# Gated delta rule and softplus block: head-pair transposes, one product for keys and queries, PSUM banks by head parity, a planner with instruction blocks, another order of loads

## Chip, cores, metric

The kernel runs on one core of a Trainium2 chip. The metric is device time in microseconds (us), the median of several executions. The engines are TensorE (PE in the profile, PEld for its weight loads), VectorE (DVE), ScalarE (ACT), GpSimd (POOL) and SyncE (SP, here only issuing DMAs). The kernel before gave 360.08 us.

## The reference

A recurrence over 768 steps for 32 heads (4 batches of 8) of width 48, then a two-layer block with softplus over all 3072 rows. Cut to what matters:

```python
B, H, S, D = 4, 8, 768, 48
k_n = k / (np.linalg.norm(k, axis=-1, keepdims=True) + 1e-06)
for t in range(S):
    y[:, :, t] = g[:, :, t] * einsum('bhd,bhde->bhe', q[:, :, t], state)
    v_old = einsum('bhde,bhd->bhe', state, kt)
    state = state + bt * einsum('bhd,bhe->bhde', kt, vt - v_old)
x = y.transpose(0, 2, 1, 3).reshape(3072, 384)
h = x @ w_in                                   # 384 -> 2048
out = (maximum(h, 0) + log1p(exp(-abs(h)))) @ w_out   # 2048 -> 384
```

## The kernel before

The sequence is cut into 6 chunks of 128 steps, each into two of 64. In a chunk: keys are normalised; keys and queries are transposed per head; products of keys with keys (for a triangular solve) and of keys with queries (for the output) are formed; a short solve runs on VectorE (first chunk) or POOL; then the recurrence over the sub-chunks, and the dense block. The order of instructions on every engine comes from a list scheduler inside the kernel ("the planner"), which is given a cost for each item.

Each matmul of the products keeps a stationary tile of 48 rows and 32 or 64 columns:

```python
def trs(...):                                   # 32 transposes of 64x64
    for j, x in ((0, a), (1, b)):               # keys, queries
        for h in range(H):
            for b2 in range(2):
                r = slice(64 * b2, 64 * b2 + 64)
                nc.tensor.transpose(o[r, h, j, :], x.ap[r, p, h, :], ident[r, r])

def kkmm(x=kqt[gi], kkp=kkp):                   # 48 matmuls, all with 32 columns
    for h in range(H):
        for b2 in range(2):
            ...
            ka, kb = x.ap[r, h, 0, :32], x.ap[r, h, 0, 32:]
            nc.tensor.matmul(o[ra, :, h, :], ka, x.ap[r, h, 0, :])   # L470
            nc.tensor.matmul(o[rb, 0, h, :], kb, kb)                 # L471
            nc.tensor.matmul(o[rb, 1, h, :], kb, ka)                 # L472

def kqmm(x=kqt[gi], mp=mp):                     # 16 matmuls, all with 64 columns
    for h in range(H):
        for b2 in range(2):
            nc.tensor.matmul(o[64 * b2 : 64 * b2 + 64, h, :],
                             x.ap[r, h, 0, :], x.ap[r, h, 1, :])     # L504
```

There are 4 such groups in a chunk, 24 in all. The two dense products are `h <- xt, w_in` (L908) and `o <- ga, w_out` (L940).

## Time and profile before

| | before |
|---|---|
| time | 360.08 us (360.02 to 362.51) |
| span of the profiled execution | 362.2 us |
| TensorE busy, matmuls | 274.1 us, 8416 |
| of these in the 24 product groups | 1152 + 384 matmuls, 0.55 and about 0.4 us a group (first start to the start of what follows; median of the groups that stand alone) |
| waits of over 0.25 us at every 128th matmul | 28, 44.9 us |
| first dense matmul | at 88.7 us |

A row of the profile's groups gives line, engine, operation, out<-in by name, stationary rows*columns, shape and count; after the first bar the time in which at least one of the group ran and the mean length of one; after the second the engine's idle time before them and who ended it. A matmul's length includes latency that overlaps with its neighbours, so what a matmul costs is read from start to start. The prediction says how the waits at every 128th matmul were found. Times of a group are measured everywhere as in the table.

### The profile page before, as it was taken

Reading aid. Unit: us, or ns where it says so; the run is one execution under the profiler, and the core shown is the slowest. Engines: PE = TensorE matmul, PEld = TensorE weight load, DVE = VectorE, ACT = ScalarE, POOL = GpSimd, SP = SyncE. Lnnn points to the kernel's source line nnn. Section 1 sums busy time; section 2 is a strip of 40 time slices with the busy share of each in tenths; the row PEclk is TensorE's granted clock in tenths of the full one; section 3 lists DMA queues with packets and bytes.
Section 4 is the critical chain, followed back from the end, with each engine's and each line's share of the span. In section 5 each row is a group of like instructions: output and inputs, shape, how many; then the busy total and the mean of one; then the engine's idle time right before and its main releaser. Section 6 shows DMA issues by size and latency. Waiting matters only on the chain.

```text
span 362.2 us, 17913 instructions
## 1 busy us (share of the span) xinstructions
PE 274.1 (76%) x8416; PEld 175.7 (49%) x8416; DVE 148.1 (41%) x280; ACT 148.9 (41%) x233; POOL 104.5 (29%) x196
## 2 busy tenths in 40 slices
PE   0351035669996897779999978985899978999984
PEld 0341034657454466435666445654565544565442
DVE  2825924239442256314566451661056330441011
ACT  3330233442775214446735674241456324541620
POOL 6400060054830892000528987000006600000000
PEclk9985555555997599569999998995599998999999
DMA  7999985714740136562416701362000011011012
GB/s 138 188 193 169 184 147 107 136 29 91 133 92 5 25 78 124 110 116 48 89 27 127 161 4 27 69 122 59 6 4 5 24 46 25 4 25 45 22 28 59
DMA packets 106473, 27.98 MB, mean 77 GB/s; under 512 B 100768, under 2 KB 106016, under 8 KB 106400
## 3 DMA queue, kind: packets, MB, share of 16 engines
q1 hardware_dynamic: 103680, 23.60, 34.0%
q0 software_dynamic: 2720, 3.24, 5.2%
q8 instruction: 65, 1.06, 1.3%
q14 instruction: 8, 0.07, 0.1%
HBM read 25.26 MB, written 4.72 MB: 83 GB/s over the span
## 4 chain that ended last, share of the span: by engine, by line
PE 71%; issue 13%; DVE 7%; ACT 5%; SPq 2%; DMA 1%; DVEq 0%; ACTq 0%
PE o L940 19%; PE h L908 19%; PE d L436 5%; PE d L752 4%; PE d L732 2%; PE d L504 2%; SPq L262 2%; ACT td L618 2%; PE d L657 2%; PE d L470 2%; PE d L637 2%; PE d L691 2%; PE d L813 2%; PE d L790 2%; PE d L824 2%
## 5 line engine op out<-in xcount | busy, mean ns | idle before, releaser
L908 PE MATMUL h<-xt,w_in 128*128 128x512 f16 x288 | 80.8, 410 | 0.8 <-DVE xt L863 0.4
L940 PE MATMUL o<-w_out,ga 128*128 128x384 f16 x384 | 75.5, 336 | 4.8 <-DVE osb L953 4.2
L922 ACT ACTIVATE ga<-h 128x512 f16<-128x512 f32 x96 | 56.8, 598 | 52.7 <-PE h L908 51.1
L744 DVE TENSOR_TENSOR w<-vf,d 128x384 f16<-128x384 f32 x48 | 25.8, 550 | 67.2 <-PE d L769 63.5
L940 PEld LDWEIGHTS <-ga 128*128 128x128 f16 x384 | 35.5, 99 | 30.6 <-issue 8.1
L368 POOL TENSOR_TENSOR ss<-ss,half_c 128x32 f32<-128x32 f32 x5 | 27.4, 5487 | 59.7 <-DVE ss L329 59.7
L761 ACT CAST u<-d 128x384 f16<-128x384 f32 x48 | 22.2, 479 | 47.9 <-PE d L752 47.9
L908 PEld LDWEIGHTS <-w_in 128*128 128x128 f16 x288 | 25.5, 102 | 27.6 <-issue 8.0
L953 DVE COPY osb<-o 128x384 f32<-128x384 f32 x24 | 13.4, 557 | 55.7 <-PE o L940 55.7
L582 POOL TENSOR_TENSOR tt<-tt,tmp 128x30 f32<-128x30 f32 (+7 forms) x75 | 29.5, 393 | 5.9
L575 POOL TENSOR_TENSOR tmp<-nn,tt 128x30 f32<-128x30 f32 (+7 forms) x75 | 28.7, 382 | 5.9
L523 DVE TENSOR_TENSOR mt<-d,mask 128x512 f16<-128x512 f32 x24 | 16.4, 683 | 29.2 <-PE d L504 29.2
L453 ACT COPY kqt<-d 128x1024 f16<-128x1024 f16 x24 | 23.8, 1014 | 9.2 <-PE d L436 9.1
L436 PE MATMUL d<-ident,kn 64*64 64x64 f16 x384 | 13.5, 219 | 17.5 <-DVE kn L389 13.9
L564 POOL TENSOR_TENSOR nn<-ln,nbeta_l 128x256 f32<-128x256 f16 x10 | 6.0, 619 | 67.4 <-DVE ln L541 67.4
L752 PE MATMUL d<-w,td 32*32 32x48 f16 x1152 | 19.4, 191 | 6.3 <-issue 4.7
L488 ACT CAST kk<-d 128x512 f16<-128x512 f32 x24 | 14.1, 586 | 23.3 <-PE d L472 23.2
L752 PEld LDWEIGHTS <-td 32*32 32x32 f16 x1152 | 14.4, 96 | 18.2 <-issue 15.3
L637 PE MATMUL d<-ident,td 32*32 32x16 f16 x768 | 7.4, 172 | 19.2 <-ACT td L618 17.7
L436 PEld LDWEIGHTS <-kn 64*64 64x64 f16 x384 | 10.6, 131 | 21.5 <-DVE kn L389 13.9
L799 DVE TENSOR_TENSOR s<-d,s 128x384 f16<-128x384 f32 x22 | 12.0, 553 | 16.4 <-PE d L790 16.4
L637 PEld LDWEIGHTS <-td 32*32 32x32 f16 x768 | 6.7, 90 | 20.8 <-ACT td L618 18.5
(69 smaller groups left out, 398.2 us busy)
## 6 DMA issues: line engine op xcount, KB each, us to landing
kf<-in_k_dram SPq DMA_DIRECT2D x24, 192.0 KB, 4.7
qf<-in_q_dram SPq DMA_DIRECT2D x24, 192.0 KB, 4.8
vf<-in_v_dram SPq DMA_DIRECT2D x24, 192.0 KB, 4.4
gf<-in_g_dram SPq DMA_DIRECT2D x24, 192.0 KB, 4.9
out_dram<-osb SPq DMA_DIRECT2D x48, 96.0 KB, 2.2
w_in<-in_moe_w_in_dram POOLq DMA_DIRECT2D x1, 1536.0 KB, 12.2
w_out<-in_moe_w_out_dram POOLq DMA_DIRECT2D x1, 1536.0 KB, 22.9
beta_l<-in_beta_dram POOLq DMA_DIRECT2D x8, 12.0 KB, 3.8
```

The costliest lines, as they stand in the source:

```text
L368: lambda ss=ss: nc.gpsimd.tensor_tensor(ss.ap, ss.ap, half_c, ALU.pow)
L436: nc.tensor.transpose(o[r, h, j, :], x.ap[r, p, h, :], ident[r, r])
L453: lambda tp=tp, o=kqt[gi]: nc.scalar.copy(o.ap.rearrange("p h j t -> p (h j t)"), f16ps(tp.ap))
L575: eng.tensor_tensor(t, nn.ap[:, :, j + 1 :, j : j + 1].broadcast_to([P, 2, n, w]), tt.ap[:, :, j : j + 1, 16 : 16 + w].broadcast_to([P, 2, ...
L582: eng.tensor_tensor(rows, rows, t, ALU.add)
L637: nc.tensor.matmul(uv(np_.ap)[r, u], td.ap[r, u, :], ident[r, 32 * qd : 32 * qd + 16],)
L744: nc.vector.tensor_tensor(o.ap, vf.ap[:, p], hd(wp.ap), ALU.subtract)
L752: nc.tensor.matmul(hd(up.ap)[r, h], td_.ap[r, u0 + 2 * h, :], o.ap[r, h],)
L761: nc.scalar.copy(o.ap, hd(up.ap))
L908: nc.tensor.matmul(hp.ap, w_in[:, j, f * P : (f + 1) * P], xt.ap[:, j, :], start=(j == 0), stop=(j == 2),)
L922: lambda hp=hp, o=gb_: nc.scalar.activation(o.ap, hp.ap, AF.Softplus)
L940: nc.tensor.matmul(op.ap[:, :DM], ga[f].ap[:, 128 * gi : 128 * gi + 128], w_out[:, f, :], start=(f == 0), stop=(f == NF - 1),)
```

## The change

Its intent is fewer instructions on TensorE. Keys and queries are transposed two heads at a time (8 transposes of 128x128 instead of 32). One matmul then gives the products of keys with keys and with queries; a second, with 32 columns, overwrites a part of its lower half. Since the two heads of a pair lie in different row halves, their products go to two PSUM banks. A second correction in the recurrence is folded into a new product z, a transposition by TensorE goes to VectorE. The planner counts matmuls in blocks of 128. The core of the diff, cuts marked with `...`, the comments behind `#` added here:

```diff
+                        for i in range(NP):
+                            nc.tensor.transpose(
+                                o[:, i, :, j],
+                                x.ap[:, p, 2 * i : 2 * i + 2].rearrange("p h d -> p (h d)"),
+                                ident,
+                            )
...
-                            nc.tensor.matmul(o[ra, :, h, :], ka, x.ap[r, h, 0, :])
-                            nc.tensor.matmul(o[rb, 0, h, :], kb, kb)
-                            nc.tensor.matmul(o[rb, 1, h, :], kb, ka)
...
+                def gram(kq=kq, gp=gp):
+                    for i in range(NP):
+                        for r in range(2):
+                            for m in range(2):
+                                x = kq.ap[FEAT[m], 2 * i + r]
+                                o = gp[m].ap.rearrange("p (i c) -> p i c", i=NP)
+                                nc.tensor.matmul(o[HALF[r], i], x[:, C:], x)        # L531
+                                o = gp[m].ap.rearrange("p (i x c) -> p i x c", i=NP, c=HC)
+                                nc.tensor.matmul(                                  # L535
+                                    o[QUAD[2 * r + 1], i, 0:3:2], x[:, C + HC :], x[:, C:]
+                                )
+                t2 = add("PE", 0.4, gram, ..., mm=32)
...
+            if e == "PE":
+                block = issued // self.BLOCK            # 128 matmuls
+                issued += it.mm
+                end = it.end
+                while issued // self.BLOCK > block:
+                    block += 1
+                    end = max(end, arrive[block])
+                    arrive.append(end + self.FETCH)     # 3.5 us
...
     load("k", k, r_k, 0)
-    for cc in range(NSS):
+    load("q", q, r_q, 0)
+    load("k", k, r_k, 1)
+    load("v", v, r_v, 0)
+    weights()                                          # w_in, planned after v of chunk 0
+    load("g", g, r_g, 0)
+    load("q", q, r_q, 1)
+    weights2()
...
```

## The prediction

> **What bounds the kernel now.** I read the page first, then the groups by line, the waits, the timeline of TensorE and the stage table.
>
> ```profile
> PE 274.1 (76%) x8416; PEld 175.7 (49%) x8416; DVE 148.1 (41%) x280; ACT 148.9 (41%) x233; POOL 104.5 (29%) x196
> q8 instruction: 65, 1.06, 1.3%
> PE 71%; issue 13%; DVE 7%; ACT 5%; SPq 2%; DMA 1%; DVEq 0%; ACTq 0%
> ...
> L908 PE MATMUL h<-xt,w_in 128*128 128x512 f16 x288 | 80.8, 410 | 0.8 <-DVE xt L863 0.4
> L940 PE MATMUL o<-w_out,ga 128*128 128x384 f16 x384 | 75.5, 336 | 4.8 <-DVE osb L953 4.2
> ```
>
> TensorE holds 71% of the chain that ended last, and another 13% (47 us) is "issue": it waits for nothing the profile shows. No other engine is busy for half of the span, so TensorE's stream is the bound. Only 672 of its 8416 matmuls are the dense ones (L908, L940). At their usual spacing in the trace (216 and 163 ns from start to start) these need 288 x 216 + 384 x 163 ns = 125 us; the remaining 7744 are small.
>
> What "issue" is shows in the timeline of TensorE from 46 to 58 us (start, length, group, count, wait before it):
>
> ```profile
> 51.52 0.66 PE L657 MATMUL d<-tn,kk 16*32 16x16 f16 x65 [2.12 <-issue]
> 52.01 0.62 PE L680 MATMUL d<-td,ident 32*32 32x512 f16 x4
> 52.92 0.59 PE L691 MATMUL d<-td,xs 32*16 32x16 f16 x59 [0.29 <-ACT xs L668]
> 55.52 0.67 PE L691 MATMUL d<-td,xs 32*16 32x16 f16 x69 [2.00 <-issue]
> 56.99 0.78 PE L752 MATMUL d<-w,td 32*32 32x48 f16 x59 [0.80 <-ACT td L704]
> ```
>
> From one "issue" wait to the next are 65 + 4 + 59 = 128 matmuls, and the wait falls in mid-group, where no data can be the reason. I numbered all weight loads: the long waits of this kind fall on number 96 modulo 128, 28 of them over 0.25 us, 44.9 us in sum. Each such block of 256 instructions goes with one packet of the instruction queue (65 packets). Blocks of small matmuls alone take 3.5 to 4.0 us however little they compute; a block with 10 or more dense matmuls has no wait.
>
> Before the steady state there is a slow start. The waits put 13.9 us down to the first normalised keys and 15.4 us to the first triangular solve on VectorE, and the first dense matmul starts only at 88.7 us.
>
> **What the Trainium skill says.** "Advanced Engine Details and Errata", section ISA Cache: lines of 16 KB, 256 instructions, two of them (it also gives TensorE more memory, which would not explain these waits). The trace agrees with the line: 1.06 MB / 65 = 16 KB, and 2 x 8416 / 256 = 65.75. "TensorEngine Tiling (Array Packing)", Key Properties: changing the tiling mode drains the array. The trace agrees: from L472 (32 columns) to L504 (64 columns) the starts are 102 to 115 ns apart every time, while L813 follows L790 (both 64 by 64) after 28 ns. Same page, Gotcha 1: different row tiles may not write one PSUM bank at once. That is why the change, which now crosses row and column halves, gives each head parity its own bank; nothing here tests it. "TensorE: Matmul & The Clock Gate", Weight-path perf modes: loads of 128 columns have a fast form. Loads of 128 columns take 99 to 105 ns here, loads of 64 columns 117 to 133, so wide transposes should not cost more for their weights.
>
> **The change part by part.** Matmuls, counted from the loops:
> - Transposes: 768 of 64x64 become 192 of 128x128. The old two rows are 13.5 + 12.7 = 26 us busy. The wide transpose of L853 follows its neighbour after 56 ns, so a group of eight takes 0.45 us and 0.1 for the mode change; 24 x 0.55 = 13 us. **-13 us.**
> - Keys and queries: 1152 + 384 become 768. The old groups last 0.55 us (48 matmuls) and about 0.5 us; 24 x 1.05 = 25 us. The new group alternates, matmul by matmul, a 64-column and a 32-column stationary tile: 32 mode changes. At the 102 to 115 ns just read, 110 ns each, a group is 3.5 us, 24 are 84 us. **+59 us.** This is the doubtful term.
> - L637 (768 matmuls, 7.4 us) goes to a VectorE transpose of 1 us per chunk; the new product z (408 matmuls) costs the same 7 us. **0.**
> - Recurrence: the second correction (wsub, umm again) is gone, the state is skipped at the start. Rows L732, L752, L769, L790, L813, L824, L853 sum to 80 us. After: 1152 matmuls of 32x32 at 19.4/1152 = 17 ns, 1440 of 64x64 at 28 ns, the 72 transposes unchanged: 20 + 40 + 9 = 69. **-11 us.**
> - Dense: same columns streamed; a warmer array may give 5 us (L908's starts average 247 ns where 216 is usual). **-5 us.**
>
> TensorE busy: 274 - 13 + 59 - 11 - 5 = 304 us.
>
> Idle: now 362 - 274 = 88 us. After: 6384 matmuls are 50 blocks, not 66, and one in four matmuls of many blocks is slow, so a fetch hides behind them; I leave 8 of 45 us. The 13 us to the first transposes stay (loads of k and q were already first). Of the 15 us behind the solve some 10 are filled, since the second chunk's normalisation moves to POOL and its products fit there: 5 left. Tail 4, other waits 8. Sum 38, hence 304 + 38 = **342 us**. The earlier dense start (I expect 55 to 65 us, because the first half chunk no longer waits for the second) is how those idle times go away; it is not a further gain. VectorE loses 24 subtractions of 0.55 us, ScalarE gains some 12 us of evictions, both stay near 150 us and off the bound. The loads move 28 MB at 150 to 190 GB/s early; their order matters for the start alone.
>
> **Rivals.**
> 1. No drain per matmul. The planner's own cost of the new group is 0.4 us, and many of its other costs sit at what this trace measures (Square 0.85 for 843 ns, the cast of q 0.60 for 629 ns), so that number may have been measured too. It leaves out things as well: it keeps 1.02 us for L618, which takes 1.97. Then the products cost 24 x 0.6 = 14 us: busy 274 - 13 - 11 - 11 - 5 = 234. Fast blocks bring fetch waits back (20 us), idle 13 + 10 + 20 + 4 + 9 = 56: **290 us**.
> 2. A full drain. When each matmul is alone in its mode its weights are not loaded ahead; the first starts of L504 are 53 ns apart from the second pair where later pairs follow after 32. With 150 ns a matmul the groups are 24 x 4.8 = 115 us: busy 335, idle 35: **370 us**, slower. For it speaks that every mode change in the trace costs about this; against it that a kernel so carefully planned would then have its largest group unseen.
> 3. PSUM becomes the wait. Products, state terms and outputs now take banks in pairs from a ring of five; products (two banks) cannot run while a step of the recurrence holds four. Only dense matmuls have banks of their own. Against it: each hold lasts a microsecond or two, and the dense work fills the gaps from 60 us on. It would add 5 to 15 us to any of the cases.
>
> **Range and chances.** The three cases for the products give 290, 342 and 370. I give them 0.3, 0.4 and 0.3, with 10 us of spread each; the point is put slightly under the middle case, at 336 us, 7% less than now. Range 288 to 372: it takes in the first and most of the third. Faster by over 2% (below 353): most of the first two and a little of the third, 0.68; within 2%: 0.17; slower: 0.15.
>
> **What would show it.** (a) The instruction queue should have about 50 packets, TensorE 6384 matmuls, and "issue" well under 13% of the chain. (b) The row of the product of keys and queries decides: starts about 110 ns apart and groups of 3.5 us mean the middle case, 12 to 16 ns the first, 150 the third. (c) Transposes of 128x128 about 56 ns apart, in groups of eight. (d) The first dense matmul by 65 us. (e) VectorE and ScalarE under 50% of the span. I am wrong if TensorE's idle time after 65 us exceeds 40 us (then banks or the recurrence bind), or if the long waits at every 128th matmul stay above 30 us in sum.

## The result

The changed kernel took **436.83 us** (435.81 to 439.71, 4 runs), before 361.11 us in the same rounds: 1.21 times as long, 95% interval 1.202 to 1.219. Ratios are the mean time of one kernel's fast runs over that of the other's of the same rounds, so not quite the ratio of the medians quoted. The result is correct. The forecast was 336 us, with a range up to 372.

The page of the changed kernel, lines that answer to those of before (busy times, instruction queue, shares of the chain that ended last, costliest groups):

```profile
PE 382.2 (88%) x6384; PEld 235.1 (54%) x6384; DVE 139.2 (32%) x278; ACT 159.4 (37%) x272; POOL 108.5 (25%) x202
...
q8 instruction: 50, 0.82, 0.9%
...
PE 81%; issue 7%; ACT 4%; DVE 3%; SPq 2%; DMA 1%; POOL 1%; ACTq 0%; POOLq 0%; DVEq 0%
...
L531 PE MATMUL d<-kqt 48*64 48x128 f16 x384 | 109.5, 285 | 1.5 <-ACT kqt L512 1.3
L1122 PE MATMUL h<-xt,w_in 128*128 128x512 f16 (+1 forms) x384 | 85.5, 369 | 0.0
L535 PE MATMUL d<-kqt 48*32 48x64 f16 x384 | 84.5, 220 | 0.0
L1160 PE MATMUL o<-w_out,ga 128*128 128x384 f16 x384 | 80.5, 355 | 2.8 <-DVE osb L1182 2.6
```

The intended things came: 6384 matmuls, 50 packets of instructions instead of 65, waits at every 128th matmul down from 44.9 to 15.5 us, "issue" 7% of the chain instead of 13%. But TensorE is busy for 108 us more with 2032 matmuls less. The first and third row, the two halves of the one product, are 768 small matmuls with 48 rows, and they hold more time than the dense block's rows.

The timeline of TensorE inside one such group (start, length, group, count):

```profile
51.85 0.31 PE L531 MATMUL d<-kqt 48*64 48x128 f16 x1
52.09 0.23 PE L535 MATMUL d<-kqt 48*32 48x64 f16 x1
52.25 0.31 PE L531 MATMUL d<-kqt 48*64 48x128 f16 x1
52.49 0.23 PE L535 MATMUL d<-kqt 48*32 48x64 f16 x1
```

Each matmul stands alone: 240 ns from the 64-column one to the 32-column one, 160 ns back. Where the granted clock is full the medians are 170 and 130 ns. Summed from start to start the 768 matmuls cost 140 us (leaving out 5 us in gaps of over 0.6 us); the two old products cost 13.0 + 9.7 = 23 us by the same rule. A whole group takes 5.5 us in the median (14 of the 24 stand alone; 140 / 24 is 5.8), where the planner was told 0.4.

The stage table for 50 to 77 us, in which TensorE does little but products (stretch, length, busy us of each engine, clock, DMA share, GB/s):

```profile
50.00:77.00 27.00, 26.75 (x141) 15.19 (x140) 10.38 (x33) 4.94 (x9) 1.99 (x2) 0.50 0.85 124
```

141 matmuls fill 27 us, and the clock is granted at half although TensorE counts as busy. The profiled execution had a mean clock of 0.756, the other three 0.85, and took the same time. Such means are not safe to compare: the records of the clock start late, here at 17.5 us, in the kernel before_wide below at 118 us, and the time before them counts as full speed, though the matmuls of before_wide run there at the pace that they have later at recorded half clock (187 ns, below). So whether the clock differed between these executions is not known. What half clock adds to the products in the profiled one is estimated further below.

### The profile page after: what moved, and what is told of

Same layout as the page of the kernel before. It is cut to its first block, busy times and chain, and to the rows that moved or that the text cites. A ratio compares the mean times of both kernels' runs of the same rounds, so it can differ in the third digit from the quotient of the medians.

```text
span 433.9 us, 13899 instructions
## 1 busy us (share of the span) xinstructions
PE 382.2 (88%) x6384; PEld 235.1 (54%) x6384; DVE 139.2 (32%) x278; ACT 159.4 (37%) x272; POOL 108.5 (25%) x202
## 4 chain that ended last, share of the span: by engine, by line
PE 81%; issue 7%; ACT 4%; DVE 3%; SPq 2%; DMA 1%; POOL 1%; ACTq 0%; POOLq 0%; DVEq 0%
PE h L1122 18%; PE d L531 17%; PE o L1160 16%; PE d L535 12%; PE d L489 3%; SPq L299 2%; PE d L843 2%; PE d L1038 2%; PE d L899 2%; PE d L954 2%; PE d L755 1%; PE d L1088 1%; PE d L997 1%; PE d L799 1%; DMA kf<-in_k_dram 1%
## 5 line engine op out<-in xcount | busy, mean ns | idle before, releaser
L531 PE MATMUL d<-kqt 48*64 48x128 f16 x384 | 109.5, 285 | 1.5 <-ACT kqt L512 1.3
L1122 PE MATMUL h<-xt,w_in 128*128 128x512 f16 (+1 forms) x384 | 85.5, 369 | 0.0
L535 PE MATMUL d<-kqt 48*32 48x64 f16 x384 | 84.5, 220 | 0.0
L553 ACT ACTIVATE kk<-d 128x256 f16<-128x256 f32 x48 | 18.1, 383 | 126.3 <-PE d L535 100.7
L572 DVE TENSOR_TENSOR mt<-d,mask 128x256 f16<-128x256 f32 x48 | 19.3, 422 | 122.7 <-ACT kk L553 93.1
L531 PEld LDWEIGHTS <-kqt 48*64 48x64 f16 x384 | 44.6, 116 | 25.8 <-issue 2.2
L535 PEld LDWEIGHTS <-kqt 48*32 48x32 f16 x384 | 36.0, 94 | 38.6 <-issue 0.3
L1160 PEld LDWEIGHTS <-ga 128*128 128x128 f16 x384 | 38.6, 105 | 30.8 <-issue 11.3
L1122 PEld LDWEIGHTS <-w_in 128*128 128x128 f16 x384 | 37.6, 106 | 26.1 <-issue 10.9
L424 POOL TENSOR_TENSOR ss<-ss,half_c 128x32 f32<-128x32 f32 (+1 forms) x6 | 27.8, 4631 | 86.1 <-DVE ss L387 86.1
L1071 DVE TENSOR_TENSOR yg<-d,gf 128x384 f16<-128x384 f32 x24 | 13.2, 553 | 54.5 <-PE d L1038 54.3
L489 PE MATMUL d<-ident,kn 128*128 128x128 f16 x96 | 13.2, 282 | 12.5 <-DVE kn L446 12.2
```

What stands on the lines that cost most here:

```text
L424: lambda ss=ss, r=r: nc.gpsimd.tensor_tensor(ss.ap[:, r], ss.ap[:, r], half_c[:, r], ALU.pow),
L489: nc.tensor.transpose(o[:, i, :, j], x.ap[:, p, 2 * i : 2 * i + 2].rearrange("p h d -> p (h d)"), ident,)
L531: nc.tensor.matmul(o[HALF[r], i], x[:, C:], x)
L535: nc.tensor.matmul(o[QUAD[2 * r + 1], i, 0:3:2], x[:, C + HC :], x[:, C:])
L553: nc.scalar.activation(kk.ap[:, :, u0 : u0 + 7 : 2].rearrange("p x i t -> p i x t"), g.ap.rearrange("p (i x t) -> p i x t", i=NP, x=4)[:, ...
L572: nc.vector.tensor_tensor(o.ap, g.ap.rearrange("p (i t) -> p i t", i=NP)[:, :, :C], mask[:, None, :].broadcast_to([P, NP, C]), ALU.mult,)
```

## The experiments

**Theory:** L531 and L535 have different tile sizes (64 and 32 stationary columns), each change of tile size empties the array, and the alternation makes 32 of them in each group. **Rival 1:** the second matmul is slow because it overwrites, with a stepped output, what the first has just written to the same bank. **Rival 2:** the rest of the change (banks in pairs, planner, loads) costs the time. All kernels below gave correct results. The second, third and fourth ran in one round, two executions each, and the record leaves their verdicts against the kernel before "unclear"; what is read from them are differences of 79 to 111 us, where two executions of one kernel lay at most 3 us apart.

### Grouping by tile size

```diff
-                    for i in range(NP):
-                        for r in range(2):
-                            for m in range(2):
-                                (64-column matmul), (32-column matmul)
+                    for f in (big, low):        # all 64-column ones, then all 32-column ones
+                        for i in range(NP):
+                            for r in range(2):
+                                for m in range(2):
+                                    f(i, r, m)
```

> The changed kernel, only the order inside the product of keys and queries is new: the 16 matmuls with 64 stationary columns first, then the 16 with 32 columns, so 2 changes of tile size in a group instead of 32; same matmuls, same schedule of everything else. Theory (each change of tile size empties the array, 145 us in all over the 24 groups of the changed kernel): a group falls from about 6 us to about 0.9 us, 24 groups to about 22 us; fetch waits at every 128th matmul come back with 15 to 20 us; the time falls from 437 to about 330 us (310 to 345), below the kernel before. Rival 1 (the second matmul is slow because it writes over what the first one just wrote in the same bank, with a stepped output): the 384 overwriting matmuls keep about 150 ns each and the time stays above 390. Rival 2 (the rest of the change, banks in pairs and the new planner, is what costs): 437 stays within 3%, because TensorE waits elsewhere.

**322.52 us** (4 runs): 0.891 of before, interval 0.886 to 0.897. The page's first line and the two rows of the product (view of groups by form):

```profile
PE 242.8 (76%) x6384; PEld 160.8 (50%) x6384; DVE 135.1 (42%) x278; ACT 157.2 (49%) x272; POOL 109.2 (34%) x202
...
L528 PE MATMUL d<-kqt 48*64 48x128 f16 x384 | 13.5, 261 | 3.8 <-ACT kqt L512 2.4 <-ACT kk L557 0.8 <-issue 0.6
...
L533 PE MATMUL d<-kqt 48*32 48x64 f16 x384 | 8.4, 211 | 0.8 <-issue 0.8
```

and its timeline:

```profile
41.27 0.64 PE L528 MATMUL d<-kqt 48*64 48x128 f16 x16 [0.25 <-ACT kqt L512]
41.85 0.40 PE L533 MATMUL d<-kqt 48*32 48x64 f16 x16
42.19 0.64 PE L528 MATMUL d<-kqt 48*64 48x128 f16 x16
42.76 0.40 PE L533 MATMUL d<-kqt 48*32 48x64 f16 x16
```

(These two groups take 0.92 us each; they lie before the first record of the clock, at 80.7 us.) The same matmuls on the same data, planned with the same costs, and a group falls from 5.5 to 0.58 us in the median. TensorE's busy time falls by 139 us, the total by 114; waits at every 128th matmul come back in part (23 us instead of 15.5). So the rest of the change is worth its place: it beats the kernel before by 11%. Rival 2 can't be the main cause of 437 us (a small part of it comes back below, under the order of loads). Rival 1 isn't excluded cleanly yet, since overwriting now comes later.

### Half as many changes of tile size

```diff
                     for i in range(NP):
                         for r in range(2):
-                            for m in range(2):
-                                (64 columns), (32 columns)
+                            for f in (big, low):    # 64, 64, 32, 32
+                                for m in range(2):
+                                    f(i, r, m)
```

> As the changed kernel, but in the order 64, 64, 32, 32 columns for each pair: 16 changes of tile size in a group instead of 32. Theory: half of the cost stays, a group about 3.2 us, 24 about 77 us instead of 145; time about 375 us (360 to 390), halfway between the changed kernel and the grouped one. If the cost were of overwriting soon after, the distance is now two matmuls instead of one and nearly all of it would stay (above 415).

357.81 us (2 runs), 79 us below the changed kernel and 0.990 of before, interval 0.981 to 0.999. The rows of the product:

```profile
L528 PE MATMUL d<-kqt 48*64 48x128 f16 x384 | 53.4, 270 | 1.9 <-ACT kqt L512 1.1 <-ACT kk L557 0.8
L533 PE MATMUL d<-kqt 48*32 48x64 f16 x384 | 41.7, 214 | 0.0
```

The groups take 2.46 us. Alternation costs 170 and 130 ns at each change as before (at the full clock), and the second matmul of each pair starts 3 ns after the first. 8 x (170 + 130) ns = 2.4 us is the whole group: the cost goes with the number of changes, not with the number of matmuls. The time is 2 us below the range that I expected; 14 of this run's 24 groups had the full clock's medians, in the changed kernel 9.

### Alternating and overwriting, but one tile size

```diff
-                                nc.tensor.matmul(o[HALF[r], i], x[:, C:], x)
+                                for h in range(2):
+                                    nc.tensor.matmul(
+                                        o[QUAD[2 * r + h], i],
+                                        x[:, C + HC * h : C + HC * h + HC], x,
+                                    )
```

> As the changed kernel with its alternating order and its immediate overwriting, but the 64-column matmul is cut in two of 32 columns: 48 matmuls a group, all of one tile size, 2 changes in a group; 6768 matmuls instead of 6384. Theory: no drain inside the group, a group about 1.0 us; time 320 to 350 us, near the grouped one. Rival 1 (overwriting in the same bank right after): the overwriting matmul keeps its 150 to 240 ns, the time stays above 390.

327.70 us (2 runs), 0.906 of before. (The planner still counts 32 matmuls for a group that now has 48.) The rows of the product:

```profile
L531 PE MATMUL d<-kqt 48*32 48x128 f16 x768 | 16.9, 245 | 6.8 <-ACT kqt L512 4.3 <-issue 2.0 <-ACT kk L557 0.4
L539 PE MATMUL d<-kqt 48*32 48x64 f16 x384 | 16.0, 212 | 2.0 <-issue 2.0
```

L539 is the unchanged overwriting matmul, still directly after the one whose output it replaces. It now starts 5 to 6 ns after its predecessor (median), and a group of 48 takes 0.57 us. Rival 1 falls. Cutting the 64-column matmul in two gives more instructions and is still 109 us faster.

### The same defect put into the kernel before

```diff
-                            nc.tensor.matmul(o[ra, :, h, :], ka, x.ap[r, h, 0, :])
+                            nc.tensor.matmul(
+                                o[64 * b2 : 64 * b2 + 64, :, h, :],
+                                x.ap[r, h, 0, :], x.ap[r, h, 0, :],
+                            )
```

> The kernel before, with one edit: in its product of keys the first of three matmuls has 64 stationary columns instead of 32 (its lower half is then overwritten by the other two, the result is the same). Same number of matmuls, same schedule, now 32 changes of tile size in each of the 24 groups. Theory: a group rises from 0.55 to about 4 us, 24 times 3.5 is 84 us more on TensorE, of which 15 to 25 us hide fetch waits: 361 becomes 415 to 440 us. Rival 2 (the rest of the change costs, not the tile sizes): stays at 361 to 370.

473.26 us (2 runs), 1.309 of before: further than the 415 to 440 expected, in the expected direction. First the three rows of the kernel before (groups of TensorE):

```profile
L470 PE MATMUL d<-kqt 48*32 48x64 f16 x384 | 13.9, 214 | 0.3 <-ACT kqt L453 0.3
L471 PE MATMUL d<-kqt 48*32 48x32 f16 x384 | 13.7, 180 | 3.2 <-issue 3.2
L472 PE MATMUL d<-kqt 48*32 48x32 f16 x384 | 13.5, 178 | 1.7 <-issue 1.7
```

then those of this kernel:

```profile
L470 PE MATMUL d<-kqt 48*64 48x64 f16 x384 | 93.3, 243 | 0.3 <-ACT kqt L453 0.3
...
L475 PE MATMUL d<-kqt 48*32 48x32 f16 x384 | 76.0, 198 | 0.0
L476 PE MATMUL d<-kqt 48*32 48x32 f16 x384 | 69.3, 181 | 0.0
```

Only the width of one stationary tile differs, and with it that the other two matmuls overwrite a part of its output, which the kernel with one tile size showed to cost nothing; a group rises from 0.55 to 5.5 us. The mean length of one matmul grows by 14% at most, the rows' busy time five- to sevenfold: what is lost is the overlap, not the speed of a matmul. The size that I expected was again too small, for the reason of the next table, of start-to-start medians at a change of tile size:

| the matmul before the change | full clock | half clock | kernel |
|---|---|---|---|
| 64 columns, 128 streamed | 170 ns | 240 ns | changed |
| 64 columns, 64 streamed | 143 ns | 187 ns | before_wide |
| 32 columns, 64 streamed | 130 ns | 160 ns | changed |
| 32 columns, 32 streamed | 103 ns | 114 ns | before_wide |

What makes up these times can be estimated from the same traces. In the alternating product the next weight load begins only with its own matmul, 170 or 240 ns after the load before it; in the grouped kernel loads begin 4 ns apart (medians). So each matmul seems to pay its weight load and its stream one after the other. Recorded loads of 64 columns last 103 ns at the full clock and 123 at half, of 32 columns 89 and 96; a stream of 128 columns takes 56 and 107 ns (the transposes' starts), one of 64 half of that. Load plus stream is then 159, 131 and 117 ns for the first three rows at the full clock, and 230, 176 and 149 at half: 10 to 13 ns under the table in all six cases. (In the fourth row the matmul isn't alone: the other one with 32 columns stands 39 to 46 ns before it.) This is arithmetic that fits, not an experiment.

### The planner alone, and without its blocks

The kernel before with the changed planner (the Plan class, counts of matmuls for each item, the costs of loads and stores), its instructions untouched:

```diff
-    def add(self, eng, cost, fn, deps=(), bufs=(), prio=0, tail=0.1, order=None):
+    def add(self, eng, cost, fn, deps=(), bufs=(), prio=0, tail=0.1, order=(), mm=0, dma=0):
...
-                    tail=0.2,
+                    tail=0.2, mm=32,
```

> The kernel before with the changed kernel's planner alone (it counts matmuls, models blocks of 128 with 3.5 us a fetch, and the loads' own time); the instructions are those of before, only their order on the engines differs. If the planner carries the gain that the grouped kernel shows over before: fetch waits at every 128th matmul fall from 45 us towards 25 and the time from 361 to about 340. If fewer matmuls carry it: the waits stay near 40 us and the time within 2% of 361. I lean to the second, with 350 to 362 us, since 66 blocks still have to be fetched.

362.74 us (4 runs), 1.006 of before: the same. Its waits at every 128th matmul sum to 45.9 us. The new planner took away none of them here, where the number of blocks is unchanged.

The grouped kernel with the planner's model of blocks off:

```diff
-    FETCH = 3.5
+    FETCH = 0.0
```

> The grouped kernel with the planner's model of instruction blocks switched off (a fetch of 0 us in the planner), all else equal. If the model of blocks carries gain, fetch waits rise from 23 us towards 35 and the time from 322 to about 330 to 335; if it does not, the time stays within 1%.

331.80 us (4 runs), ratio to before 0.920 against 0.891: about 9 us, or 3%, as expected. The waits at every 128th matmul rose less than I thought, to 26.3 from 23 us, so how the other 6 us are lost is not shown.

### The order of loads

In the grouped kernel, the loads of k, q, v, g in the order of before:

```diff
     load("k", k, r_k, 0)
-    load("q", q, r_q, 0)
-    load("k", k, r_k, 1)
-    load("v", v, r_v, 0)
-    ... (first two chunks by hand)
+    for cc in range(NSS):
+        load("q", q, r_q, cc)
+        load("v", v, r_v, cc)
+        if cc == 0:
+            weights()
+        if cc == 1:
+            weights2()
+        if cc + 1 < NSS:
+            load("k", k, r_k, cc + 1)
+        load("g", g, r_g, cc)
```

> The grouped kernel with the loads of k, q, v, g in the order of before (the weights still issued after v of chunk 0 and q of chunk 1). The DMA engines are full for the first 75 us in both, and the first dense matmul needs the same bytes in either order; so I expect no change over 1.5% (318 to 327 us). If the new order was worth its place, the time is over 327.

313.90 us (308.20 to 317.05, 4 runs): below the 318 to 327 us expected, though its runs spread so far (three lie over 1.5% above the fastest) that no ratio with an interval is formed. And in the changed kernel itself, the alternating product left in:

> The changed kernel with its alternating product untouched, only the loads of k, q, v, g in the order of before. In the grouped kernel this order saved some 8 us. Here TensorE is full of the alternating products from 17 to 77 us, before the first dense matmul at 97.8 us, so the loads should be hidden: 437 us within 2%. If it fell below 425, the order of loads would have been a cause of its own for the slow result.

422.47 us (4 runs), 1.180 of before where the changed kernel had 1.211: a miss. I had expected the loads to be hidden. So the new order, with what it does to the load of w_in, is a second, small cause of the slow result: 0.03 of before by the two ratios, or 11 us (14 between the medians, which are from different rounds). Between the two orders the trace shows one more difference: POOL works in order, and the load of w_in left its queue at 11.3 us with the old order, at 23.9 us in the grouped kernel and at 32.5 us in the changed one, behind the first work for the second chunk. Two more kernels tried to separate the two: the new order with w_in planned after q of chunk 0 (issued ahead of that work), and the old order with w_in planned after g of chunk 0 (behind it). The traces show that the edits did this: w_in left at 10.9 and at 27.4 us.

```diff
-                deps=[tiles["v", 0, 1][1]],
+                deps=[tiles["q", 0, 1][1]],
```

> The grouped kernel with its own new order of loads, but the first weight load placed on POOL's queue ahead of the work for the second chunk (as it came to stand when the loads had the old order: issued at 11 us there, at 23.9 us in the grouped run). If the gain of the old order (322 to 314 us) came from the weights leaving POOL's queue earlier, this one takes 312 to 317 us; if it came from the order of k, q, v, g, it stays at 320 to 325.

319.19 us (4 runs, one of them slow), 0.888 of before: between the two outcomes that I had expected.

```diff
-                deps=[tiles["v", 0, 1][1]],
+                deps=[tiles["g", 0, 1][1]],
```

(with the call moved after the load of g)

> The grouped kernel with the old order of k, q, v, g, but the first weight load placed after g of the first chunk, behind POOL's first work for the second chunk. If the early issue of the weights made the gain, the time returns to 319 to 325 us; if the order of k, q, v, g did, it stays at 310 to 317.

321.84 us (4 runs), 0.900 of before. With the late weights the old order of loads has no gain left; with early weights the new order has at best 1%. Both seem needed together, but in the grouped kernel the differences are of the size of the runs' spread, so that a gain of the old order is clear of noise in the changed kernel only; why the two would need each other stays open.

### A wait on ScalarE that cost nothing

In the grouped kernel ScalarE stood before the squaring of the third chunk's keys, with the first solve's copy behind it (timeline of ScalarE):

```profile
51.07 1.08 ACT L675 CAST tn<-tn 128x512 f16<-128x512 f32 x1 [3.26 <-DVE tn L665]
57.10 0.84 ACT L380 ACTIVATE ksq<-kf 128x768 f32<-128x768 f32 x1 [4.95 <-DMA kf<-in_k_dram]
57.85 1.94 ACT L695 CAST td<-t 128x1024 f16<-128x1024 f32 x1
```

```diff
                 deps=[kl],
                 bufs=[kf, ksq],
                 prio=pl + 4,
+                order=[l4s[cc - 2]] if cc >= 2 else (),
```

> The grouped kernel, but ScalarE's squaring of the keys of chunk c is placed only after the solve's copy of chunk c-2. In the grouped run ScalarE, which runs in order, stood at 57.1 us before the squaring of the third chunk's keys, whose load had not landed, and the copy of the first solve behind it waited from about 52 to 57.8 us. If that wait is on the path to the first dense matmul (74.2 us), it comes 4 to 6 us sooner and the time falls to about 317; if the loads bind there anyway, the time stays within 1% of 322.

322.02 us (4 runs), 0.892 of before: no gain. The first dense matmul came at 72.1 instead of 74.2 us, but in the profiled execution the waits at every 128th matmul came to 28.6 instead of 23.3 us.

### The fastest version run with enough rounds

The grouped kernel, the old order of loads, and two planner costs set to the traces:

```diff
-                    0.4,          # gram
+                    0.6,
...
-            1.02,                 # copy of the solve
+            1.95,
```

> The grouped kernel with the loads in the order of before, and two costs of its planner set to what the traces show (the grouped product 0.6 us instead of 0.4, the copy of the solve 1.95 us instead of 1.02); the instructions are the same, their order may differ. The grouped kernel with the old order of loads took 308 to 317 us in four runs; with truer costs I expect 305 to 316 us, 12 to 15% under before. If the planner's costs don't matter, it stays at 314 within 1%. The faster of the two orders is what I would keep.

316.49 us (6 runs), 0.883 of before, interval 0.880 to 0.887; expected were 305 to 316. The truer costs alone are not shown to help: the kernel without them had 313.9 us in other rounds.

## Why the prediction was wrong

**The step that failed is the second of the change's parts, "Keys and queries", with its +59 us.** Its mechanism was right as far as the runs test it (each change of tile size costs, and the overlap of neighbours is lost there), the size was not. It took 110 ns for a matmul, read from a change after a matmul with 32 columns that streamed 32. The new matmuls stream 128 and 64 and keep 64 columns in every second case, and each takes 130 to 170 ns at the full clock and 160 to 240 at half. From start to start the products cost 140 instead of 23 us, **+117 us**. Rival 2 had named a reason that the traces agree with (weights not loaded ahead) and a step of 150 ns, which is the mean of the two directions at the full clock; over the whole run the mean is 140 us / 768 = 183 ns, because most of the groups ran at half the clock (an estimate: 768 x 150 ns = 115 us, the other 25 us from the clock). I then set the range by giving the case without drains 0.3, because the planner's 0.4 us might have been measured. The experiments show that it can hold for a grouped product only (0.58 us), and that nobody's list of costs is evidence against a wait that the trace shows at every change.

**The other terms of TensorE's busy time** (304 forecast, 382 measured). Rows overlap, so sums of them are a rough account:
- Transposes, -13 us forecast: 26.2 became 26.4 us by the rows of the page. I had set a start-to-start sum beside a row's busy time, which aren't the same quantity, and used 56 ns, which the trace after has at the full clock only (107 at half, 106 in the median of all). Nothing was gained by this measure.
- Recurrence, -11 us: the rows that take its place sum to 56 instead of 80 us, -24.
- Dense, -5 us: the two rows went from 156 to 166 us, +10.
- Against the forecast these are: products +58, transposes +13, dense +15, recurrence -13, in sum +73 of the 78 us missed. The solve's products, forecast at 0, account for most of the rest: their rows went from 26.7 to 33.3 us.

**Idle time:** 52 instead of 38 us. The waits at every 128th matmul are 15.5 us, not 8, and the first dense matmul came at 97.8 us, not by 65: the second chunk's products, each group 5.5 us, stood before it. In the grouped kernel it is 74.2 us, where the DMA engines are full for the first 70 us, so even without the defect it would not have come by 65.

**Its signs of being wrong** did not fire: TensorE's idle time after 65 us was 32 us (limit 40), the waits at every 128th matmul 15.5 us (limit 30). Both watch idle time; the error lay in busy time, in the one term that the prediction had called doubtful. The test that it named as the deciding one, (b), came out beyond its worst case: 183 ns a matmul in the mean, against 150. One reading is a little too smooth: of the 22 blocks with 10 or more dense matmuls one does have a wait, of 0.46 us.

**What was right:** the bound (TensorE), instruction blocks of 128 matmuls with one packet each (65 to 50), fetches hidden behind slow products, VectorE and ScalarE off the bound. Of the three cases rival 1 (290 us) is the nearest to what the change is without its defect, 314 to 323, but still 24 to 33 us too low. Rival 3, PSUM banks, was tested by no kernel of its own; the grouped kernel leaves it little room. The rule on row tiles that the prediction quotes is not quite untested: in the kernel before, both row halves of L470 to L472 write one tile of one bank, in different partitions, with 48 starts in 0.43 us, and the result is correct. In the new layout both row halves would write the same partitions; that no run tries.

What each wide transpose saves against the old form, and the value of the fold of the second correction alone, were not run.

## What to carry to other kernels

Count changes of tile size on TensorE as you count instructions: here 32 in a group cost ten times the group's work, and putting matmuls of one size together took 114 us off without changing one of them. When a wait is priced from a trace, take it from the case with the same weights, the same size of stream and the same clock, or add what differs. A scheduler's cost that has not been read from a run is an intention, so compare planned and measured time group by group before looking elsewhere.

## What the Trainium skill lacked or had wrong

- "TensorEngine Tiling (Array Packing)", Key Properties: it says that changing the mode drains, but gives no cost, and no page prices a change. Runs: 103 to 170 ns from start to start at the full clock, 114 to 240 ns at half; it grows with the columns streamed. Inside one mode the medians are 3 to 20 ns in the other product groups, and 39 to 46 ns between the two matmuls with 32 columns of before_wide.
- "Runtime: NRT & Kernel Launch", Instruction fetch mechanics: it calls the cost of crossing a line of 256 instructions mostly hidden; "Advanced Engine Details and Errata", ISA Cache, gives no cost. Before, 11 of the 20 blocks of 128 matmuls with no dense one among them took 3.5 to 4.0 us each, and the waits at the boundaries were 44.9 us in sum.
- "TensorE: Matmul & The Clock Gate": sustained work should lift the clock. In the changed kernel TensorE was busy for 26.75 of 27 us by the profile, with alternating small matmuls, and was granted 0.50 of the clock throughout; its matmuls' pace agrees (240 ns where they take 170 at the full clock).
